# A two-layer attention and GEGLU kernel: memory denominators folded into the numerators' products, a reordered head, zeroing on GpSimd, four-bank exponentials, and a new order

## The chip, the cores and the metric

The kernel runs on one core of a Trainium2 chip. The time is device microseconds of one execution of the whole program; three runs of the kernel before gave 535.21, 535.64 and 536.88 us, a median of 535.64. One more execution was profiled. Where the text speaks of an engine, PE is TensorE (matmuls), PEld its weight loads, DVE is VectorE, ACT is ScalarE, POOL is GpSimd, and SP is the engine that issues most DMAs.

## The reference, cut to what matters

Two layers, each an attention with a compressive memory and then a gated FFN, over 2048 rows of width 512, in bfloat16.

```python
def attention(x):                       # H = 32 heads of Dh = 16, four segments of L = 512 rows
    for s in range(4):                  # one after the other: the memory is carried on
        logits = qs @ ks.T * scale + causal_mask
        a_dot = softmax(logits) @ vs
        pq = phi(qs)                    # phi(t) = t + 1 if t > 0 else exp(t)
        num = pq @ M                    # M: Dh x Dh for each head
        den = pq @ z + 1e-06            # z: Dh for each head
        o = g * (num / den) + (1 - g) * a_dot
        pk = phi(ks)
        M = M + pk.T @ vs
        z = z + pk.sum(rows)
    return concat(o) @ wo

def ffn(x):
    return gelu(x @ w_gate) * (x @ w_up) @ w_down      # inner width 1792

x = x + attention(layernorm(x))
x = x + ffn(layernorm(x))
x = x + attention(layernorm(x))
x = x + ffn(layernorm(x))
```

## The kernel before

All weights and x stay in SBUF. The work is cut into eight stages k = 0 to 7: layer one's four segments of 512 rows, then layer two's. In each stage stand the projections q, k, v (`qk`, `v`), 36 rounds of scores with their exponentials and the products of the probabilities with v (`score_round`, `flush_item`), the memory (`mem_items`, and `upd_item` which adds this segment to it), the output projection `wo`, and the FFN's `gate`, `up` and `down` products.

The heads have 16 channels, so a block of 128 channels holds eight heads. The program uses TensorE in three arrangements: `whole` (one 128x128 product), `rows` (four products side by side, one for each 32 channels: the scores) and `columns` (four products of 32 output rows each: the probabilities with v, and any dense product that happens to be issued beside them). `product` chooses `whole` or `columns` for a dense product by what stands ahead of it. A dense product is one step of 512 columns (or four steps side by side that together take the time of one).

**What sets the order.** The kernel has no hand-written sequence. The function `order` is a planner that runs while the program is built: it keeps a clock for each engine, a list of items that are ready (`Item`, each with a due time, its matmuls and what follows them), and emits the instructions in the order in which its clocks would run them. The table `POLICY`, with `STAGES` that change it in windows of 20 us of the planner's time, gives the due times, the slack of each kind of post-processing, and which engine may take a job that two or three can do. So each engine has a fixed program afterwards, and waits for others by semaphores. Where no item is ready and rounds of scores are still to come, the planner emits a small product of the tile `warm` (128 columns) as a filler.

**PSUM** is one tile `ps` of eight banks of 512 float32. An item takes one bank (`Psum`), a pair of score rounds takes two pairs of neighbouring banks, and `exp` in `score` reads one pair in one ACT instruction of 1024 elements (line 1864 of the profile). `pick` chooses a bank, `banks` holds when each comes free.

**The memory before.** After the update of stage k the tile `mblk` (four blocks of 128x128, with M on the block diagonal, made by one DVE product with the 0/1 tile `bd`, line 1286) and the tile `zcols` (four blocks of 128x8, one column for each head, line 1292) are built. In stage k + 1, `den` runs 16 products of 8 columns each into one bank (`den_mm`), DVE adds 1e-06 and multiplies by the gate (line 1195) and takes the reciprocal of 128 values (line 1200) into `rdm`; then four items `num`, one for each block of 128 channels, run four products of 128 columns each into a bank, and DVE multiplies each by `rdm` into `am` (line 1226). `am` is transposed by a DMA into `amT`, and added to the attention's output at line 1417. This happens in the six stages that have a memory.

**Other places that the change touches.** In the head, one matmul of a single row broadcasts `beta` to all partitions, between the first products of k and q. `kx` holds k with one half of its channels zeroed; its zero part is set by two DVE memsets of 1024 words (lines 707 and 709), `masked_copies` fills the rest. `vaug` is v with one more column for each head, for the softmax's sum; its column is written once by DVE (line 698). The norm's transposed rows `xnT` come from a DMA transpose or from TensorE (`turn_item`, four products with the tile `ident` and one PSUM eviction), as `turn_pe` and `turn_last` say. The last `down` item of each stage of layer two is split in two halves of 256 columns, each with its own addition to x (line 1463) and its own DMA to the output.

Of the kernel before, what the change touches and what calls it, by code (L numbers as in the profile page):

```python
# [10 lines left out]
ACT = mybir.ActivationFunctionType  # L11
ALU = mybir.AluOpType
# [20 lines left out]
SCALE = DH ** -0.5  # L33
EPS_LN = 1e-5
# [31 lines left out]
def table(halved):  # L66
# [17 lines left out]
    if halved:  # L84
# [31 lines left out]
    rs_pool=32.757, f_urge=-233.244, quick=2, paired=8, turn_pe=1, turn_last=0, w_at=29.345, w_gap=2.17,  # L116
    wd_at=78.552, wd_gap=2.776, flush_wait=-13.887, piece_slack=40.254, kb_slack=24.368, mem_slack=-20.134,
    margin=0.5, qk_due=0.962, e_q=49.408, e_k=2.993, exp_slack=-6.401, e_slack=131.01, phi_slack=22.785,
    gelu_slack=-0.789, act_evict=1.671, first_evict=0.248, gate_step=93.832, up_due=-100.529, up_step=84.355,
    down_due=-29.196, down_step=-47.297, upd_due=91.807, kb_act=82.777, vz_slack=55.93, x_dve=2.467, v0_due=-11.641,  # L120
    x1_at=-87.497, x2_at=16.051, x3_at=24.107, x3_load=-378.834, direct=2, gelu_tiles=0, look=3, lag=0.852,
    wv_at=-320.502, xn_pool=19.822, kb_pool=121.576, cut_pool=154.009, at_pool=-238.466, pe_turns=0, gate_due=4.191,
    shun=8.799, col_gap=0.807, hold=5, early=104.615, starve=0.16, near=114.234, cap=13, soon=28.208, columns=0,
    kd_slack=-5.85, zero_slack=-1.031, hold1=-49.923, hold2=2.205, hold3=11.541, hold_step=-162.485, hold_v=23.995,
    park=3)

STAGES = [
    (1, 2, dict(
        rs_pool=0.722, quick=9, kb_slack=2.193, mem_slack=-24.231, e_q=-2.643, gelu_slack=-0.49, gate_step=79.021,
        up_due=-101.483, up_step=41.973, down_step=-58.4, upd_due=91.729, vz_slack=33.291, direct=8, gelu_tiles=2,  # L130
        lag=0.412, at_pool=-237.424, early=83.209, starve=60.426, soon=7.146, park=4)),
    (2, 3, dict(
        rs_pool=2.667, quick=6, turn_pe=0, kb_slack=55.298, mem_slack=-32.756, e_q=-2.851, gelu_slack=-0.49,
        gate_step=78.038, up_due=-98.977, up_step=25.491, down_step=-53.827, upd_due=91.729, vz_slack=14.093,
        x_dve=7.459, direct=6, gelu_tiles=2, look=2.764, lag=0.475, xn_pool=30.206, cut_pool=102.189,
        at_pool=-237.424, gate_due=8.415, starve=1.292, soon=7.146, park=5)),
    (3, 4, dict(
        rs_pool=4.794, turn_pe=12, kb_slack=51.509, mem_slack=58.674, e_q=50.036, e_k=1.445, gelu_slack=1.935,
        gate_step=78.038, up_due=-96.513, up_step=85.14, down_step=-56.495, vz_slack=40.138, x_dve=6.187, direct=6,
        look=2.618, xn_pool=30.206, cut_pool=118.125, at_pool=-208.534, gate_due=14.291, shun=21.0, early=101.394,  # L140
        starve=0.321, soon=7.146, park=2)),
    (4, 5, dict(
        rs_pool=-2.341, quick=0, turn_pe=12, kb_slack=85.554, mem_slack=58.674, qk_due=1.009, e_q=50.137, e_k=1.464,
        gelu_slack=0.429, gate_step=79.294, up_due=-96.513, up_step=84.505, down_step=-72.139, vz_slack=51.333,
        x_dve=6.187, direct=3, gelu_tiles=2, xn_pool=20.238, cut_pool=148.746, at_pool=-208.534, gate_due=8.415,
        shun=21.0, early=101.394, starve=0.453, soon=7.146, park=2)),
    (5, 6, dict(
        rs_pool=36.794, quick=0, turn_pe=12, kb_slack=66.017, mem_slack=58.674, qk_due=1.009, e_q=55.15, e_k=2.984,
        gelu_slack=-0.805, gate_step=79.294, up_due=-96.513, down_step=-70.89, vz_slack=18.865, x_dve=7.455,
        gelu_tiles=2, look=2.835, lag=0.71, xn_pool=20.238, cut_pool=148.746, at_pool=-208.534, gate_due=0.276,  # L150
        shun=21.488, soon=7.146)),
    (6, 7, dict(
        rs_pool=11.417, f_urge=-261.392, quick=0, paired=11, turn_pe=0, flush_wait=0.581, piece_slack=36.524,
        kb_slack=76.591, mem_slack=-10.427, qk_due=-0.609, e_q=97.288, e_k=-5.757, exp_slack=-18.942, e_slack=69.536,
        phi_slack=30.587, gelu_slack=0.965, act_evict=1.166, gate_step=33.55, up_due=-80.509, down_due=-55.61,
        down_step=-81.567, upd_due=143.06, kb_act=60.08, vz_slack=4.039, x_dve=18.331, direct=0, gelu_tiles=2,
        look=2.622, lag=0.754, xn_pool=-3.088, kb_pool=116.679, cut_pool=153.155, at_pool=-189.709, gate_due=0.226,
        shun=85.539, hold=8, early=169.131, starve=0.31, near=101.522, cap=11, soon=0.694, kd_slack=37.99, park=6)),
    (7, 8, dict(
        rs_pool=-52.581, f_urge=-61.761, quick=3, paired=0, turn_pe=13, flush_wait=-3.039, piece_slack=92.516,  # L160
        kb_slack=220.906, mem_slack=57.517, qk_due=-30.647, e_q=-54.782, e_k=89.983, exp_slack=-17.861,
# [411 lines left out]
def order(pol, nc, cst, seg, wrk, psp, A_x, A_wq, A_wk, A_wv, A_wo, A_beta, B_x, B_w_gate, B_w_up, B_w_down, out):  # L573
# [185 lines left out]
    class Psum:  # L759
# [6 lines left out]
        def read(self, t):  # L766
            banks[self.bank] = t + 0.05
# [1239 lines left out]
```

## Time and profile before

| | |
|---|---|
| median of three runs | 535.64 us |
| span of the profiled execution, first to last instruction | 533.3 us |
| PE busy | 524.7 us, 98% |
| DVE busy | 434.6 us, 81% |
| ACT busy | 445.8 us, 84% |
| POOL busy | 252.5 us, 47% |
| DMA queue q1 | 28.20 MB, 25.8% of 16 engines' span |

The median of the runs lies 2.4 us over the profiled span. A matmul's busy time in the trace lasts from its start to its modelled end, and the next one starts long before that: a product of 512 columns is busy for 380 ns, while the starts of two that follow each other are 0.215 us apart. So PE's busy share says only that it seldom stood still; what a piece of PE's work costs is read from the starts in the timeline, as the time from a group's first start to the next group's. "issue" behind an idle time means that nothing that the profile shows was waited for.

### The profile page before, as it was taken

The page shows a single profiled execution, that of the slowest core. Times are in us where ns is not written, and L with a number is a line of the kernel's source. Part 1 is how long each engine was busy: PE and PEld are TensorE (multiplying, and loading weights), DVE is VectorE, ACT ScalarE, POOL GpSimd, SP SyncE. Part 2 cuts the span into 40 slices and gives each one's busy share as a digit, 9 for nine tenths or more (in the row PEclk, how much of TensorE's full clock was granted, in tenths as well). Part 3 has the DMA queues.
Part 4 walks back from the last instruction along what each step waited for, and adds up shares of the span by engine and source line. Part 5 has one row for each costly group of instructions (what it writes and reads, how often), then busy time and mean ns, then how long its engine had stood idle before and what let it go on. Part 6 is the DMA issues. An engine that isn't in the chain of part 4 may idle for free.

```text
span 533.3 us, 24180 instructions
## 1 busy us (share of the span) xinstructions
PE 524.7 (98%) x10697; PEld 275.7 (52%) x10697; DVE 434.6 (81%) x836; ACT 445.8 (84%) x598; POOL 252.5 (47%) x320
## 2 busy tenths in 40 slices
PE   9999989999999999999999999999999999999997
PEld 4454455444545455555564454555555456555544
DVE  7899997999997999889987788888976997586342
ACT  6999989888999989899898899799979988952320
POOL 2987472548541966428773366391632254400000
PEclk9999999999999999999999999999999999999999
DMA  8367750333330232101221122410250132102101
GB/s 271 76 120 148 190 158 4 69 39 77 42 69 16 53 56 38 32 12 25 53 41 31 25 32 27 60 33 2 53 102 3 33 51 53 23 2 48 37 2 41
DMA packets 76762, 29.99 MB, mean 56 GB/s; under 512 B 61042, under 2 KB 76658, under 8 KB 76658
## 3 DMA queue, kind: packets, MB, share of 16 engines
q1 hardware_dynamic: 76368, 28.20, 25.8%
q8 instruction: 83, 1.36, 1.0%
q10 hardware_dynamic: 290, 0.26, 0.1%
q14 instruction: 21, 0.17, 0.1%
HBM read 9.70 MB, written 2.10 MB: 22 GB/s over the span
## 4 chain that ended last, share of the span: by engine, by line
PE 75%; DVE 5%; ACT 3%; POOL 1%; issue 1%; DMA 1%; ACTq 0%
PE ps L541 75%; ACT pt L1864 1%; DVE xn L920 1%; DVE st L856 1%; ACT gel_sb L1616 1%; POOL kx L726 1%; DVE x_sb L1463 1%; ACT gel_sb L1519 1%; POOL e L1170 1%; DMA xnT<-xn 1%; ACT gel_sb L779 0%; DVE ab L1407 0%; DVE byq L1391 0%; DVE aT L1414 0%; DVE x_sb L869 0%
## 5 line engine op out<-in xcount | busy, mean ns | idle before, releaser
L1864 ACT ACTIVATE pt<-ps 128x1024 bf16<-128x1024 f32 x288 | 279.0, 1036 | 27.5 <-PE ps L541 18.6
L1813 POOL TENSOR_SCALAR_AFFINE_SELECT pt<-pt 128x256 bf16<-128x256 bf16 (+1 forms) x192 | 112.4, 598 | 176.4 <-ACT pt L1864 173.9
L541 PE MATMUL ps<-xnT,wg_sb 128*32 128x512 bf16 (+3 forms) x1367 | 107.7, 362 | 0.2 <-DMA xnT<-xn 0.2
L541 PE MATMUL ps<-wd_sb,gel_sb 128*32 128x512 bf16 (+2 forms) x1431 | 106.1, 354 | 0.0
L541 PE MATMUL ps<-xnT,wu_sb 128*32 128x512 bf16 (+1 forms) x1252 | 103.5, 379 | 0.2 <-ACT gel_sb L1519 0.2
L1557 DVE TENSOR_TENSOR gel_sb<-gel_sb,ps 128x512 bf16<-128x512 bf16 x112 | 75.2, 684 | 30.2 <-PE ps L541 27.9
L541 PEld LDWEIGHTS <-gel_sb 128*32 128x32 bf16 (+1 forms) x1623 | 53.0, 97 | 41.4 <-issue 2.2
L541 PEld LDWEIGHTS <-wu_sb 128*32 128x32 bf16 (+1 forms) x1252 | 45.6, 97 | 45.4 <-issue 2.1
L541 PEld LDWEIGHTS <-wg_sb 128*32 128x32 bf16 (+1 forms) x1367 | 47.4, 97 | 38.7 <-issue 1.4
L1391 DVE STREAM_TRANSPOSE byq<-ps 128x512 f32<-128x512 f32 x64 | 45.3, 709 | 24.0 <-PE ps L541 23.3
L1170 POOL TENSOR_SCALAR e<-e 128x512 bf16<-128x512 bf16 x32 | 49.5, 1550 | 7.0 <-ACT e L1147 6.4
L1463 DVE TENSOR_TENSOR x_sb<-x_sb,ps 128x512 bf16<-128x512 bf16 (+1 forms) x54 | 34.1, 636 | 17.9 <-PE ps L541 17.8
L1818 POOL TENSOR_SCALAR_AFFINE_SELECT pt<-pt 64x1024 bf16<-64x1024 bf16 x32 | 38.5, 1203 | 20.7 <-ACT pt L1864 17.4
L541 PE MATMUL ps<-xnT,wk_sb 128*32 128x512 bf16 (+2 forms) x330 | 34.8, 377 | 0.7 <-ACT pt L1864 0.7
L541 PE MATMUL ps<-pt,vaug 128*32 128x256 bf16 (+2 forms) x1344 | 35.1, 239 | 0.1
L541 PE MATMUL ps<-xnT,wq_sb 128*32 128x512 bf16 (+2 forms) x339 | 34.0, 377 | 0.0
L1616 ACT ACTIVATE gel_sb<-gel_sb 128x1024 bf16<-128x1024 bf16 (+4 forms) x31 | 33.3, 1157 | 0.0
L541 PE MATMUL ps<-wv_sb,xnT 128*32 128x512 bf16 (+1 forms) x227 | 32.4, 380 | 0.8 <-DVE x_sb L1463 0.4
L541 PE MATMUL ps<-q,kx 32*128 32x64 bf16 (+2 forms) x1120 | 31.6, 217 | 0.6 <-ACT pt L1864 0.3
L541 PEld LDWEIGHTS <-vaug 128*32 128x32 bf16 x1344 | 27.1, 97 | 9.2 <-issue 1.6
L856 DVE BATCH_NORM_STATS2 st<-x_sb 128x6 f32<-128x512 bf16 x46 | 31.3, 680 | 0.4
L541 PEld LDWEIGHTS <-kx 32*128 32x128 bf16 x1120 | 17.0, 92 | 28.2 <-issue 27.4
(127 smaller groups left out, 708.7 us busy)
## 6 DMA issues: line engine op xcount, KB each, us to landing
vz<-vaug SPq DMA_DIRECT2D x14, 136.0 KB, 2.9
wg_sb<-in_B_w_gate_dram SPq DMA_DIRECT2D x8, 224.0 KB, 2.9
wu_sb<-in_B_w_up_dram SPq DMA_DIRECT2D x8, 224.0 KB, 3.9
wd_sb<-in_B_w_down_dram SPq DMA_DIRECT2D x7, 256.0 KB, 5.9
x_sb<-in_A_x_dram SPq DMA_DIRECT2D x3, 512.0 KB, 6.7
out_dram<-x_sb SPq DMA_DIRECT2D x12, 128.0 KB, 1.9
xnT<-xn SPq DMA_TRANSPOSE x56, 2.6
kx<-kf SPq DMA_DIRECT2D x12, 64.0 KB, 3.2
```

The source lines that it names most:

```text
L541: self.nc.tensor.matmul(*args, **kw)
L726: return lambda: eng.tensor_scalar(out=kx[:, :, C * which:C * which + n], in0=kf[:, :, 0:n], scalar1=masks[:, which:which + 1], scalar2=No ...
L856: nc.vector.bn_stats(out=self.st6[:, 0, :], in_=x_sb[:, self.tt0 + j, :])
L920: eng.tensor_scalar(out=xn[:], in0=x_sb[:, self.tt0 + j, :], scalar1=self.mv[:, j, 1:2] if self.wide else self.mv[:, j, 0:1], scalar2=self ...
L1170: lambda eng: eng.tensor_scalar(out=e[0][:], in0=e[0][:], scalar1=1.0, scalar2=None, op0=ALU.min), summed)
L1391: nc.vector.transpose(out=(self.byq[:, pars[0], :, :].rearrange("p a c -> p (a c)") if h is None else self.byq[:].rearrange("p u a c -> p ...
L1463: ck.dve.post(ck.made(), slack, (0.15 + 0.00104 * (c1 - c0), lambda: nc.vector.tensor_tensor(out=xt, in0=xt, in1=ps()[:, 0:c1 - c0], op=AL ...
L1557: ck.dve.post(ck.made(), NORMAL, (0.683, lambda: nc.vector.tensor_tensor(out=g, in0=g, in1=ps()[:], op=ALU.mult), lambda t: (ps.read(t), e ...
L1616: return (0.205 + 0.427 * (f1 - f0), lambda: nc.scalar.activation(out=g, in_=g, func=ACT.Gelu_apprx_tanh), lambda t: self.gelu_done(t, f0, ...
L1813: nc.gpsimd.affine_select(out=view, in_=view, pattern=[[0, 4], [0, n], [1, C]], compare_op=ALU.is_ge, fill=0.0, base=C, channel_multiplier=-1)
L1818: nc.gpsimd.affine_select(out=view, in_=view, pattern=[[0, 4 * TPS], [1, C]], compare_op=ALU.is_ge, fill=0.0, base=0, channel_multiplier=-1)
L1864: nc.scalar.activation(out=pt_all[:, s0:s0 + 2, 2 * p:2 * p + 2, :].rearrange("p r h c -> p h r c"), in_=ps_all[:, pair[0]:pair[1] + 1, :] ...
```

## The change

Denominators: the tiles `mblk` and `zcols` become one tile `mz` of four blocks of 128x136, in which each head has its 16 columns of M and one column of z. The 16 products `den_mm` are gone. The numerators' products are 136 columns wide and give the sums too. Since three blocks of 136 fit into a bank, and four don't, the four items `num` become three, of which two hold six products and one four; each takes a pair of neighbouring banks (`Pair`, `wide`). DVE then adds 1e-06 and multiplies by the gate for each item (one instruction, or two), takes a reciprocal of 48 or 32 values, and multiplies (one instruction, or two). `mz` is filled by four DVE instructions instead of one.

```diff
-                    product(ps()[:, j * P:(j + 1) * P], self.phiq[:, b, j * P:(j + 1) * P], mem_state[k - 1][0][:, b, :])
+            parts = [((0, 0, None), (1, 4, 0)), ((2, 0, None), (1, 4, 1)), ((3, 0, None),)]
+                ps = Pair()
+                    product(ps()[:, i, MZ * u:MZ * u + MZ], self.phiq[:, b, j * P:(j + 1) * P], mem_state[k - 1][0][:, b, :])
...
+                    steps = [(0.175, den(whole, 0, 2, 0, 4), None)]
+                    if half:
+                        steps.append((0.157, den(1, 2, 3, 4, 6), None))
+                    steps.append((0.454 if half else 0.354, inverse, None))
+                    if half:
+                        steps.append((0.42, scale(1, 2, 3, 4, 6, 2 * n, 2 * n + 2), None))
+                    steps.append((0.69, scale(whole, 0, 2, 0, 4, 0, TPS), told))
```

Head, zeroing and columns: `beta_row` has 128 rows, all zero but the first, and its product runs with the full tile `warm` behind the first product of q; the zero part of `kx` is set by GpSimd at the start; GpSimd may take the columns of `vaug` too.

```diff
-    beta_row = cst.tile([1, H], BF16, name="beta_row")
+    beta_row = cst.tile([P, H], BF16, name="beta_row")
+    nc.gpsimd.memset(beta_row[:], 0.0)
...
+    for kx in kxs:
+        nc.gpsimd.memset(kx.bitcast(mybir.dt.uint32)[:, :, :, C // 2:3 * C // 2], 0)
...
     a0.first_k(ps1, 0, half)
-    te.matmul(beta_ps, lhsT=warm[0:1, :], rhs=beta_row[:], start=True, stop=True)
     a0.first_q(ps2, 0, half)
+    te.matmul(beta_ps, lhsT=warm[:], rhs=beta_row[:], start=True, stop=True)
```

Four-bank exponentials: where four neighbouring banks are free, and at least `join` more, both pairs of a score round are read by one ACT instruction of 2048 elements. In the program made, this happens four times; 280 exponentials of two banks are left of 288.

```diff
+        joined = bool(runs) and len(got) - 4 >= pol.join
...
+                nc.scalar.activation(
+                    out=pt_all[:, s0:s0 + 2, :, :].rearrange("p r h c -> p h r c"),
+                    in_=ps_all[:, b0:b0 + 4, :].rearrange("p h (r c) -> p h r c", r=2), func=ACT.Exp, scale=SCALE)
```

The last `down` item of a stage of layer two is split into 384 and 128 columns, and `POLICY` and `STAGES` hold new numbers throughout, so the order on every engine is another.

```diff
-                downs[-1:] = [down(TPS - 1, 0, D // 2), down(TPS - 1, D // 2, D)]
+                downs[-1:] = [down(TPS - 1, 0, D - P), down(TPS - 1, D - P, D)]
...
-    rs_pool=32.757, f_urge=-233.244, quick=2, paired=8, turn_pe=1, turn_last=0, w_at=29.345, w_gap=2.17,
+    rs_pool=-104.717, f_urge=-62.078, quick=7, paired=14, turn_pe=0, turn_last=0, w_at=29.345, w_gap=1.105,
```

Counted over the whole programs:

| | before | changed |
|---|---|---|
| products of 8 columns for the denominators (whole, and groups of four in columns) | 64 + 32 | 0 |
| products for the numerators (whole, and groups of four) | 67 + 29, 128 columns | 28 + 68, 136 columns |
| TensorE transposes of xn (`ident`) | 32 | 48 |
| DMA transposes of xn | 56 | 52 |
| filler products of 128 columns (whole, and groups of four) | 11 + 2 | 0 + 3 |
| changes between the three arrangements | 292 | 301 |
| all dense products of q, k, v, wo, gate, up, down | the same | the same |
| ACT gelu instructions over kept tiles | 31 | 17 |
| DVE instructions | 798 | 858 |

Three places show how the instructions moved. The first is DVE at the memory of stage 1, before: `rdm` are the denominators, `am` the scaled numerators, `ab`, `aT` and `byq` belong to the attention of the stage before, `gel_sb` lines to the FFN.

```order
L1407 TENSOR_TENSOR ab<-byq,r 128x2x16x16
L1195 SCALAR_TENSOR_TENSOR rdm<-ps,tmp_e_135 128x128
L1200 RECIPROCAL rdm<-rdm 128x128
L1557 TENSOR_TENSOR gel_sb<-gel_sb,ps 128x512 x3
L1226 TENSOR_TENSOR am<-ps,rdm 128x512 x2
L1557 TENSOR_TENSOR gel_sb<-gel_sb,ps 128x512 x3
```

The same place on DVE in the changed program (line numbers are its own):

```order
L742 CAST gel_sb<-ps 128x512
L1186 SCALAR_TENSOR_TENSOR rdm<-ps,tmp_e_138 128x32
L1186 SCALAR_TENSOR_TENSOR rdm<-ps,tmp_e_138 128x16
L1194 RECIPROCAL rdm<-rdm 128x48
L1201 TENSOR_TENSOR am<-ps,rdm 128x256
L1201 TENSOR_TENSOR am<-ps,rdm 128x512
```

One denominator pass for the stage, followed by four multiplications spread between other work, has become three runs of sums, reciprocal and multiplications, and all of a run stands between the matmuls that fill a pair of banks and the moment that the pair comes free.

The second place is PE at the end of stage 0, where the rows of the first FFN's norm are turned on TensorE (`ident`), before: `wv_sb` is a projection of v, `warm` a filler, `kx` a round of scores.

```order
L541 MATMUL ps<-wv_sb,xnT 128x512
L541 LDWEIGHTS warm
L541 MATMUL ps<-warm 128x128
...
L545 LDWEIGHTS xn
L545 MATMUL ps<-ident,xn 128x128
...
L541 LDWEIGHTS kx_123
L541 MATMUL ps<-q,kx_123 128x64
```

And in the changed program:

```order
L498 LDWEIGHTS xnT
L498 MATMUL ps<-wv_sb,xnT 128x512
...
L502 LDWEIGHTS xn
L502 MATMUL ps<-ident,xn 128x128
...
L498 LDWEIGHTS wg_sb
L498 MATMUL ps<-xnT,wg_sb 128x512
```

Before, eleven fillers stand around the last transposes, and the gate's first products come after a round of scores and the memory's update; now the last eight transposes follow a projection of v and the gate's first products follow them, with no filler.

The third place is the end of the program, on DVE, before (`x_sb` lines add a `down` product to x):

```order
L1557 TENSOR_TENSOR gel_sb<-gel_sb,ps 128x512 x14
L1463 TENSOR_TENSOR x_sb<-x_sb,ps 128x512 x3
L1463 TENSOR_TENSOR x_sb<-x_sb,ps 128x256 x2
```

And in the changed program:

```order
L1559 TENSOR_TENSOR gel_sb<-gel_sb,ps 128x512 x14
L1465 TENSOR_TENSOR x_sb<-x_sb,ps 128x512 x2
L1465 TENSOR_TENSOR x_sb<-x_sb,ps 128x384
L1465 TENSOR_TENSOR x_sb<-x_sb,ps 128x128
L1465 TENSOR_TENSOR x_sb<-x_sb,ps 128x512
```

The split item is no longer the last one: behind its 128 columns comes a whole item of 512.

More of the change, by code (lines that the diff above doesn't have):

```diff
@@ L531, in __init__ @@
         self.posted, self.chain = 0.0, False
[L532 removed]
+        self.early, self.rest, self.stop, self.wide = None, None, 0, False
 class Products:
@@ L1806, in open_item @@
         items.remove(it)
+        if it.wide:
+            bank = min(free_pairs(), key=lambda p: max(banks[p[0]], banks[p[1]]))[0]
+            banks[bank + 1] = 1e9
         it.ps.bank = bank
@@ L1921, in order @@
             for ck.back in (pol.lag, 0.0):
-                got = [it for it in items if it.after in ev and it.ready() and (
+                got = [it for it in items if it.after in ev and (not it.wide or free_pairs()) and it.ready() and (
                     it.kind != "flush" or it.chain or not streams or tight() or it.posted < late or ck.mode == "columns")]
```

521 lines of the change are left out of this document (261 added, 260 removed).

## The prediction

> **What bounds the kernel now.** First the page: which engine is busy, and what the chain that ended last is made of.
>
> ```profile
> span 533.3 us, 24180 instructions
> PE 524.7 (98%) x10697; PEld 275.7 (52%) x10697; DVE 434.6 (81%) x836; ACT 445.8 (84%) x598; POOL 252.5 (47%) x320
> PE 75%; DVE 5%; ACT 3%; POOL 1%; issue 1%; DMA 1%; ACTq 0%
> ```
>
> PE is the engine that sets the end. The other engines are four fifths busy, near enough to matter where they are late, but a microsecond more on DVE or ACT costs nothing by itself. Next the busy time by stretches, to see where PE stood still and at what clock.
>
> ```profile
> core 0: us, PE busy (x) PEld busy (x) DVE busy (x) ACT busy (x) POOL busy (x), PEclk, DMA share, GB/s
> 0.00:20.00 20.00, 18.77 (x134) 8.88 (x135) 15.91 (x49) 15.59 (x32) 10.17 (x23) 1.00 0.71 204
> 20.00:40.00 20.00, 19.68 (x386) 10.09 (x388) 17.66 (x38) 19.89 (x31) 17.34 (x23) 1.00 0.54 107
> 40.00:60.00 20.00, 19.28 (x486) 10.26 (x475) 17.84 (x34) 19.92 (x25) 13.39 (x19) 1.00 0.75 165
> 60.00:80.00 20.00, 18.28 (x361) 9.70 (x359) 18.56 (x39) 17.42 (x30) 12.04 (x13) 1.00 0.59 165
> 80.00:100.00 20.00, 19.78 (x364) 10.04 (x366) 15.37 (x27) 19.50 (x24) 3.84 (x7) 1.00 0.12 29
> 100.00:140.00 40.00, 39.30 (x858) 19.55 (x851) 37.91 (x78) 34.27 (x48) 27.29 (x32) 1.00 0.35 56
> 140.00:200.00 60.00, 59.47 (x1189) 30.96 (x1188) 54.72 (x108) 57.02 (x77) 32.25 (x39) 1.00 0.25 48
> 200.00:300.00 100.00, 99.85 (x1984) 53.56 (x1983) 86.82 (x157) 90.37 (x111) 54.52 (x66) 1.00 0.16 31
> 300.00:400.00 100.00, 99.90 (x2194) 52.71 (x2193) 84.11 (x160) 90.49 (x124) 52.86 (x64) 1.00 0.27 44
> 400.00:480.00 80.00, 80.00 (x1736) 42.27 (x1738) 63.56 (x111) 69.09 (x82) 28.84 (x40) 1.00 0.15 28
> 480.00:533.00 53.00, 50.36 (x1044) 27.71 (x1036) 22.13 (x42) 12.27 (x23) 0.00 (x0) 1.00 0.13 32
> ```
>
> The granted clock is 1.00 throughout, so no term below has a clock in it. PE's idle time outside the first and last rows is 0.32 + 0.72 + 1.72 + 0.22 + 0.70 + 0.53 + 0.15 + 0.10 = 4.5 us; the largest piece, 1.72 us, lies between 60 and 80 us. These are the visible gaps; a gap that is shorter than a matmul's pipelined rest is hidden in the busy time. So there are two ways to make this kernel faster: less work on PE, worth its time directly, and fewer gaps, worth 4.5 us and a little more. The largest gap's stretch, in PE's timeline:
>
> ```profile
> 66.24 0.40 PE L541 MATMUL ps<-q,kx 32*128 32x64 bf16 x20
> 66.57 0.82 PE L541 MATMUL ps<-wv_sb,xnT 128*128 128x512 bf16 x3
> 67.23 0.61 PE L545 MATMUL ps<-ident,xn 128*128 128x128 bf16 x8
> 67.68 1.03 PE L541 MATMUL ps<-wv_sb,xnT 128*128 128x512 bf16 x4
> 68.54 0.33 PE L541 MATMUL ps<-warm 128*128 128x128 bf16 x3
> 71.58 0.29 PE L541 MATMUL ps<-q,kx 32*128 32x64 bf16 x7 [0.26 <-ACT pt L1864]
> 74.56 0.29 PE L541 MATMUL ps<-q,kf 16*128 16x64 bf16 x7
> 76.09 0.36 PE L541 MATMUL ps<-q,kf 16*128 16x192 bf16 x5 [1.24 <-issue]
> ```
>
> Fillers run at 68.54; at 71.58 PE waits for an exponential, and before 76.09 it stands for 1.24 us for nothing that the profile shows. The same rows give prices, from start to start. Four products of 512 columns take 68.54 - 67.68 = 0.86 us, 0.215 each. A transpose takes (67.68 - 67.23) / 8 = 0.056. The twenty score products from 66.24 are five groups of four side by side, four of 64 columns and one of 256, together the columns of one 512 product; they last 0.33 us, so the change of arrangement behind them is worth about 0.33 - 0.215 = 0.11 us.
>
> **The change, part by part.** *Denominators on PE.* Two of the six blocks, one in columns and one whole:
>
> ```profile
> 89.76 0.68 PE L541 MATMUL ps<-zcols,phiq 128*32 128x8 bf16 x64
> 90.28 0.84 PE L541 MATMUL ps<-xnT,wu_sb 128*32 128x512 bf16 x12
> 145.06 0.55 PE L541 MATMUL ps<-zcols,phiq 128*128 128x8 bf16 x16
> 145.47 1.67 PE L541 MATMUL ps<-xnT,wg_sb 128*128 128x512 bf16 x7
> ```
>
> A block takes 0.52 us in columns and 0.41 whole. With 32 groups in columns (two blocks) and 64 whole products (four blocks) that is 2 x 0.52 + 4 x 0.41 = 2.7 us, all gone. The numerators' 96 steps grow by 8 columns; at 0.215 us for 512 columns that is 96 x 8 x 0.00042 = 0.3 us added. Of all terms this is the surest, because PE has no slack to hide it.
>
> *Denominators on DVE.* The rows:
>
> ```profile
> L1226 DVE TENSOR_TENSOR am<-ps,rdm 128x512 bf16<-128x512 f32 x24 | 15.9, 678 | 1.0 <-PE ps L541 1.0
> L1200 DVE RECIPROCAL rdm<-rdm 128x128 f32<-128x128 f32 x6 | 5.7, 953 | 0.2
> L1195 DVE SCALAR_TENSOR_TENSOR rdm<-ps,tmp_e 128x128 f32<-128x128 f32 x6 | 1.7, 278 | 0.0
> L1401 DVE RECIPROCAL r<-byq 128x32 f32<-128x32 f32 x32 | 11.3, 354 | 1.1
> L1463 DVE TENSOR_TENSOR x_sb<-x_sb,ps 128x256 bf16<-128x256 bf16 x8 | 3.3, 418 | 3.9 <-PE ps L541 3.9
> ```
>
> Before: 6 x (0.278 + 0.953) + 24 x 0.678 = 23.7 us. Now: 30 narrower additions of at most 0.278 (I take 0.2), 12 reciprocals of 48 values between 0.354 and 0.953 (on the line between them, 0.45), 6 of 32 at 0.354, 18 multiplications at 0.678 and 12 half ones at the 0.418 of the other 256-wide row: 6.0 + 5.4 + 2.1 + 12.2 + 5.0 = 30.7 us, 7 us more. It is hidden behind PE as long as nobody waits for it: 434.6 + 7 is still 83% of the span. If that cover is gone, the price is the wait for banks, below.
>
> *Arrangements and transposes.* The order has 301 changes of arrangement against 292: 9 x 0.11 = +1.0 us. It has 16 more TensorE transposes: 16 x 0.056 = +0.9 us. Four DMA transposes less save PE nothing.
>
> *Head.* The one-row product of beta:
>
> ```profile
> 7.68 0.60 PE L541 MATMUL ps<-xnT,wk_sb 128*128 128x256 bf16 x4
> 8.21 0.18 PE L541 MATMUL ps<-beta_row,warm 1*128 1x32 bf16 x1
> 8.33 1.05 PE L541 MATMUL ps<-xnT,wq_sb 128*128 128x256 bf16 x8
> ```
>
> From 7.68 to 8.33 are 0.65 us for 1056 columns, which at 0.00042 us are 0.44: 0.2 us go to the arrangement of one row. With 128 rows they are saved: -0.2. The zeroing on POOL and the columns there take work from DVE in the first 40 us, where DVE isn't the bound; I cost them at nothing, between -0.2 and +0.2 (POOL's work from its start to 20 us is 10.17 us, so there is room).
>
> *Four-bank exponentials.* Four times one instruction of 2048 elements for two of 1024. ACT may gain or lose some tenths at each and the first pair's banks come free up to one exponential later; four of 144 rounds, nothing.
>
> *Tail.* Now the last item is a whole one:
>
> ```profile
> 527.35 0.69 DVE L1463 TENSOR_TENSOR x_sb<-x_sb,ps 128x512 bf16<-128x512 bf16 x1 [2.33 <-PE ps L541]
> 530.41 0.42 DVE L1463 TENSOR_TENSOR x_sb<-x_sb,ps 128x256 bf16<-128x256 bf16 x1 [1.11 <-PE ps L541]
> out_dram<-x_sb SPq DMA_DIRECT2D x12, 128.0 KB, 1.9
> out_dram<-x_sb SPq DMA_DIRECT2D x8, 64.0 KB, 1.9
> ```
>
> The addition behind the last matmul takes 0.69 instead of 0.42 us, and the last DMA 1.9 either way: +0.3.
>
> *Sum of what can be counted:* -2.7 + 0.3 + 1.0 + 0.9 - 0.2 + 0.3 = -0.4 us. The folding, worth 2.4 us alone, is nearly spent on arrangements and transposes.
>
> *Gaps.* The new order decides the rest. Its only sign outside the clock is the fillers, which stand where nothing was ready: 11 + 2 before, 3 now, and none where the first FFN begins. I take the gain as this place alone: the 1.72 us of idle between 60 and 80 us and eleven fillers at 0.056, together -2.3 us, and leave the other gaps as they are. The bounds are all 4.5 us of gaps and the fillers, -5.1, and on the other side the waits for banks, +4.9.
>
> So the span goes from 533.3 to 533.3 - 0.4 - 2.3 = 530.6 us; the runs' median lies 2.4 us over the profiled span, which gives **532.9 us**, 0.5% less.
>
> The 1.24 us gap has a rival reading. In this row the DMA queue of the instructions fetches 16 KB blocks, one each 533 / 83 = 6.4 us:
>
> ```profile
> q8 instruction: 83, 1.36, 1.0%
> ```
>
> If the gap is a block that came late beside the weight loads (165 GB/s in that stretch), the new order runs into the same late block and saves 1.24 us less: 532.9 + 1.2 = 534.1. The Trainium skill (Runtime: NRT & Kernel Launch, section Instruction fetch mechanics) says that fetching is hidden, since instructions are dispatched more slowly than blocks are filled; by that rule the gap is something else in this order, and the 532.9 holds. No row here shows what PE waited for.
>
> **The rivals.** *Only the count shows (no gap is won).* The new order moves the gaps instead of closing them: 535.6 - 0.4 = 535.2 us. For it: the other engines are as busy as before, ACT at 19.9 of 20 us until 60 us, and the same exponentials must be done. Against: no fillers are left there.
>
> *Banks (slower).* A numerator item now holds two neighbouring banks until DVE has done a whole run: two additions, a reciprocal and two multiplications, 0.4 + 0.45 + 0.418 + 0.678 = 2.0 us for twelve of them, 0.2 + 0.354 + 0.678 = 1.2 us for six; before, one bank was held for 0.678. The additional hold is 12 x 1.3 + 6 x 0.5 = 19 us on a pair, plus what queues ahead on DVE. Behind a bank wait are dense products and, through the pairs, score rounds, and ACT with them. If a quarter of it shows as waiting PE, that is +4.9 us, and with the count and no gap won 535.6 - 0.4 + 4.9 = 540.1. It decides from 2.0 us on, 0.11 us for each of the 18 items, if no gap is won. The Trainium skill (TensorEngine Tiling (Array Packing), section Gotcha 1: PSUM Pressure) warns that row tiling raises the pressure on PSUM because its tiles write to different banks; that is why four banks go with each score round here. Against this rival: six banks are left beside a pair, and PE waits for ACT's or DVE's banks only for tenths in the rows above.
>
> *All gaps close:* 535.6 - 0.4 - 5.1 = 530.1 us. Against: some of these gaps are chains through norm and transposes that no order removes.
>
> **How the numbers follow.** Chances: the forecast with its neighbourhood, 531.0 to 534.0, 0.50; all gaps close, 0.12; only the count, with the late block's 534.1, 0.20; banks or a new wait like them, 0.18. A measurement of this kernel can't tell less than 0.3%, 1.6 us, from no change: faster means below 534.0, slower above 537.2. So faster is 0.50 + 0.12 = 0.62, the same 0.20, slower 0.18. The range is 529.5, just under all gaps closed, to 538.0, which takes in a mild form of the bank wait; beyond it I leave about 0.1 above and less below. The forecast's own range is 531.0 to 534.0.
>
> **What would show it.** The denominators' 8-column products are gone and the products of `mz` start about 0.058 us apart in both arrangements, which confirms the first term; if they start further apart, it is wrong. Between 60 and 80 us PE's idle should fall from 1.72 to under 0.5 us; if it doesn't, the gap term is wrong and the time is 535. The sum of idle over 20 to 480 us should be about 2.7; if it is over 6, with waits of PE for `am` or for the exponentials behind the pairs of banks, the bank rival has it. The last addition takes 0.69 us. DVE should be busy for 435 to 447 us.

## The result, and the profile after

The changed kernel is slower: 554.70 us, the median of four runs (553.64 to 556.98), against 536.05 for the kernel before on the same chip. The ratio is 1.036 with an interval of 1.032 to 1.040. The forecast was 532.9, with a range up to 538.0. The profiled execution took 554.22 us, with a span of 552.5. Its page, first lines and the chain that ended last, by engine:

```profile
span 552.5 us, 24098 instructions
...
PE 526.9 (95%) x10652; PEld 271.2 (49%) x10652; DVE 433.7 (78%) x899; ACT 442.3 (80%) x590; POOL 244.4 (44%) x316
...
PE 67%; ACT 15%; DVE 8%; issue 4%; DMA 4%; POOL 1%; SPq 0%; ACTq 0%; DVEq 0%; POOLq 0%
```

PE's busy time hardly moved (524.7 before, 526.9 now). The 19.2 us that the span grew by are nearly all idle PE: 552.5 - 526.9 = 25.6 us against 8.6. The other engines did the same work and were idle longer too, so none of them became the bound; in the chain PE's share fell from 75% to 67%, and what took its place are ACT, DVE and DMAs that PE waited for. By stretches, with the columns of the prediction's view (span of the stretch, busy us of PE, PEld, DVE, ACT and POOL, clock, DMA):

```profile
40.00:60.00 20.00, 18.15 (x341) 8.69 (x343) 16.15 (x30) 18.25 (x25) 10.72 (x14) 1.00 0.76 174
60.00:80.00 20.00, 17.00 (x390) 8.79 (x386) 17.31 (x32) 18.03 (x23) 13.00 (x18) 1.00 0.43 127
...
140.00:200.00 60.00, 56.69 (x1072) 28.44 (x1070) 47.20 (x103) 47.08 (x62) 27.52 (x30) 1.00 0.21 34
200.00:300.00 100.00, 96.38 (x1958) 49.48 (x1958) 81.94 (x169) 87.32 (x119) 44.62 (x55) 1.00 0.20 37
300.00:400.00 100.00, 94.83 (x2063) 48.06 (x2065) 81.68 (x179) 83.57 (x110) 50.89 (x63) 0.98 0.20 37
```

The loss isn't at one place. From 200 to 400 us, where PE had stood still for 0.25 us in the kernel before, it now stands for 3.62 + 5.17 = 8.8 us. What it waited for, over the whole execution (us in total, times, longest), is the next view:

```profile
PE ps L498 <- DMA xnT<-xn: 9.7, 7, 2.6
PE ps L498 <- issue: 2.3, 1, 2.3
PE ps L498 <- ACT pt L1876: 2.1, 4, 1.1
PE ps L498 <- POOL pt L1824: 1.5, 1, 1.5
...
PE ps L498 <- ACT gel_sb L743: 1.0, 1, 1.0
PE ps L498 <- DMA phik<-e: 0.7, 1, 0.7
...
PE ps L502 <- DVE am L1201: 0.6, 1, 0.6
```

Before, the line for the DMAs that write `xnT` was this one:

```profile
PE ps L541 <- DMA xnT<-xn: 0.2, 1, 0.2
```

So 9.5 of the 17.0 us of new idle time, over half, are PE waiting for the transposed rows of a norm. The longest of these waits, in PE's timeline, and under it the DMAs on SP's queue in the same stretch:

```profile
336.08 0.70 PE L498 MATMUL ps<-vaug,phik 128*32 128x32 bf16 x64
336.60 0.25 PE L498 MATMUL ps<-warm 128*32 128x128 bf16 x4
339.47 1.05 PE L498 MATMUL ps<-wv_sb,xnT 128*32 128x512 bf16 x16 [2.62 <-DMA xnT<-xn]
```

```profile
335.23 6.19 SPq L711 DMA_TRANSPOSE xnT<-xn  x4
```

SP began to issue the four transposes of this norm at 335.23 and was through with the last at 341.4. PE had come to the values' product of the first block of these rows at 336.85 and stood 2.62 us until that block had landed. In these traces PE's products run in the order of the program, so all that was placed behind it stood too. The wait was made by the order: the product was put there too early.

**The numbers in the new table that do this.** The table's full text holds two numbers that the shortened diff above doesn't show. `margin` is added to the time at which the planner takes a DMA transpose as landed; it was 0.5 us everywhere. `lag` is taken off PE's time when the planner asks whether an input is there; it lay between 0.0 and 1.4.

```diff
-    margin=0.5, ...                                  (whole table; lag from 0.004 to 1.414)
+    margin=-4.735, ...                               (base)
+    margin 0.5, 0.5, 1.409, 0.297                    (planner's 0 to 80 us)
+    margin=-5.965 ... -2.498 ... -56.548 ... -4.811  (stretches behind it)
+    lag=-32.215, -31.838, -46.448                    (planner's 40 to 100 us; 0.85 to 37.9 elsewhere)
```

With a margin of -4.7 a transpose counts as landed as soon as SP has issued it. In the stretch above the first block landed 4.2 us after its issue had begun, and 2.62 us of that show as PE's wait.

**How far the chip falls behind the plan.** The planner has a clock of its own, by which it places every instruction; it is code of the kernel and no measurement. Set against the trace, matmul by matmul in program order, it shows where the chip loses time that the planner did not count on; the time that the planner itself leaves empty ("holes") is in both and drops out. In us, chip minus plan, the median of the matmuls around each time of the trace, and at the end the span minus the planner's last time:

```
at us of the trace     40    80   120   160   200   250   300   350   400   450   500    end
kernel before         0.3   1.1   1.4   2.5   2.9   2.9   2.9   2.7   2.9   2.7   2.7    4.9   (plan 528.4)
the change           -0.1   4.2   4.2   9.6   9.4  10.7  13.8  18.9  20.0  20.4  21.4   25.1   (plan 527.4)
```

By the planner's clock the change gains 1.0 us. On the chip it falls back by 20.2 us more than the kernel before, in steps at the waits listed above.

### The profile page after: what moved, and what is told of

Read it like the earlier page. It is cut to its first block, busy times and chain, and to the rows that moved or that the text cites. A ratio compares the mean times of both kernels' runs of the same rounds, so it can differ in the third digit from the quotient of the medians.

```text
span 552.5 us, 24098 instructions
## 1 busy us (share of the span) xinstructions
PE 526.9 (95%) x10652; PEld 271.2 (49%) x10652; DVE 433.7 (78%) x899; ACT 442.3 (80%) x590; POOL 244.4 (44%) x316
## 4 chain that ended last, share of the span: by engine, by line
PE 67%; ACT 15%; DVE 8%; issue 4%; DMA 4%; POOL 1%; SPq 0%; ACTq 0%; DVEq 0%; POOLq 0%
PE ps L498 66%; ACT pt L1876 7%; DMA xnT<-xn 4%; ACT gel_sb L1618 3%; ACT gel_sb L1521 2%; DVE x_sb L1465 1%; ACT L540 1%; ACT e L1111 1%; DVE byq L1393 1%; DVE xn L884 1%; POOL xn L884 1%; DVE x_sb L833 0%; DVE st L820 0%; DVE gel_sb L1559 0%; DVE phiq L1115 0%
## 5 line engine op out<-in xcount | busy, mean ns | idle before, releaser
L1876 ACT ACTIVATE pt<-ps 128x1024 bf16<-128x1024 f32 x280 | 267.5, 1043 | 31.8 <-PE ps L498 28.1
L1819 POOL TENSOR_SCALAR_AFFINE_SELECT pt<-pt 128x256 bf16<-128x256 bf16 (+1 forms) x192 | 114.5, 610 | 206.5 <-ACT pt L1876 181.1
L498 PE MATMUL ps<-xnT,wg_sb 128*32 128x512 bf16 (+2 forms) x1451 | 107.4, 378 | 6.8 <-issue 2.3
L498 PE MATMUL ps<-xnT,wu_sb 128*32 128x512 bf16 (+1 forms) x1210 | 105.0, 380 | 0.6 <-DVE gel_sb L1559 0.4
L498 PE MATMUL ps<-wd_sb,gel_sb 128*32 128x512 bf16 (+4 forms) x1497 | 103.1, 357 | 0.0
L1465 DVE TENSOR_TENSOR x_sb<-x_sb,ps 128x512 bf16<-128x512 bf16 (+2 forms) x51 | 32.4, 636 | 22.0 <-PE ps L498 21.8
L1824 POOL TENSOR_SCALAR_AFFINE_SELECT pt<-pt 64x1024 bf16<-64x1024 bf16 x24 | 28.5, 1188 | 12.3 <-ACT pt L1876 10.6
L498 PE MATMUL ps<-wo_sb,aT 128*32 128x512 bf16 (+1 forms) x311 | 31.3, 380 | 0.0
L820 DVE BATCH_NORM_STATS2 st<-x_sb 128x6 f32<-128x512 bf16 x43 | 29.2, 678 | 0.3
```

The costliest lines, as they stand in the source:

```text
L498: self.nc.tensor.matmul(*args, **kw)
L820: nc.vector.bn_stats(out=self.st6[:, 0, :], in_=x_sb[:, self.tt0 + j, :])
L1465: ck.dve.post(ck.made(), slack, (0.15 + 0.00104 * (c1 - c0), lambda: nc.vector.tensor_tensor(out=xt, in0=xt, in1=ps()[:, 0:c1 - c0], op=AL ...
L1819: nc.gpsimd.affine_select(out=view, in_=view, pattern=[[0, 4], [0, n], [1, C]], compare_op=ALU.is_ge, fill=0.0, base=C, channel_multiplier=-1)
L1824: nc.gpsimd.affine_select(out=view, in_=view, pattern=[[0, 4 * TPS], [1, C]], compare_op=ALU.is_ge, fill=0.0, base=0, channel_multiplier=-1)
L1876: nc.scalar.activation(out=pt_all[:, s0:s0 + 2, 2 * p:2 * p + 2, :].rearrange("p r h c -> p h r c"), in_=ps_all[:, pair[0]:pair[1] + 1, :] ...
```

## The experiments

**Theory M**: `margin` is the cause; the planner places products ahead of rows that have not landed. **L**: `lag` is. **B**: the code is (the pairs of banks, the new products, the zeroing on POOL). **D**: any table but the old one falls behind like this.

*1. margin put back in the changed table, e1_after_margin.*

```diff
-    margin=-4.735, ... margin=-5.965, ... margin=-4.811 (13 places)
+    margin=0.5 (all)
```

> The changed kernel with one number of its table put back: margin, which is added to the time at which the planner takes a DMA transpose as landed, is 0.5 everywhere as in the kernel before (the changed table has -4.735, -4.811, -5.965, -56.548 and others). Theory M (the planner is told that transposed rows land some 5 us early, and puts TensorE's products ahead of them): TensorE's wait on the DMAs that write xnT falls from 9.7 us to under 2 us and no dip of the granted clock is left. The order that results has more holes, filled with transposes of ident (about 180 such rows against 3), so the sum of streaming and changes of arrangement rises by about 13 us, and the time is 542 to 552 us. Theory L (lag, the other number that moves a product against its input, is the cause) and theory B (banks held in pairs): the wait on the DMAs stays at 7 us or more, and the time is 560 us or more, since the holes come on top.

Measured: 591.38 us, ratio 1.103 [1.099, 1.107]. That is far above the 542 to 552 us of theory M, and the wait on `xnT` fell to 7.4 us in two pieces, not to under 2. By the letter this is what was forecast for theories L and B: a wait of 7 us or more, and over 560 us.

```profile
PE ps L498 <- ACT pt L1876: 10.3, 17, 4.5
PE ps L498 <- DMA xnT<-xn: 7.4, 2, 5.7
```

But the planner's clock now ends at 580.7, 53 us later, where 13 had been expected: the table's other numbers were chosen with the false margin, and without it the planner itself finds holes. Against its plan the chip behaves as theory M says: it is 4.9 us behind at 120 us and 5.5 at 500, where the change went from 4.2 to 21.4. The 5.7 us wait stands in the plan as well (at 540 us the chip is 5.7 us behind). The waits alone don't tell planned holes from surprises; the distance to the plan does, and the next runs are read by it.

*2. The false margin in the kernel before, e2_before_margin.* Code and all other numbers unchanged.

```diff
-    margin=0.5, qk_due=0.962, ...
+    margin=-4.8, qk_due=0.962, ...
```

> The kernel before, code and table, with margin -4.8 in place of 0.5. Theory M: TensorE's wait on the DMAs that write xnT rises from 0.2 us to 6 to 12 us, in gaps of 0.5 to 3 us in front of products that read xnT, and the time from 536 us to 543 to 552 us (order alone: 12 more changes of arrangement and 4 more fillers, about 1.5 us). Theories L, B and D (the new code, or other numbers of the table): the wait stays under 2 us and the time is 536 to 539 us.

Measured: 552.82 us, 1.032 [1.028, 1.036], 0.8 us above the range given; this is as slow as the change, with nothing of its code. The plan ends at 533.4, 5.0 us later than unaltered, and the chip is 17.4 us behind it, 12.5 us more. The wait is in the expected range:

```profile
PE ps L541 <- DMA xnT<-xn: 7.8, 9, 2.1
```

So one number is enough to make such a loss, and the new code isn't needed for it.

*3. The new code with the old table, e3_code_alone.* `join` and `col_pool`, which the old table lacks, are set so that no four-bank exponential is formed and the columns stay on DVE; `margin` is 0.6.

> The changed kernel's code with the table of the kernel before (margin 0.6). Theory B (the paired banks, the new products or the masked k on GpSimd stall TensorE): waits for pt and am of 5 us or more in all, and 550 us or more. Theory M: TensorE waits on xnT's DMAs under 1.5 us, on the evictions of the pairs under 3 us; the old numbers suit the new code badly and leave holes (about 134 fillers against 13, some 6 us), so 540 to 545 us, well under the 554 us of the change.

Measured: 566.35 us, 1.056 [1.053, 1.060]. By the letter this is theory B's result: over 550 us, and the waits for `pt` are 7.8 us.

```profile
PE ps L542 <- ACT pt L1920: 7.2, 15, 1.4
...
PE ps L542 <- DMA xnT<-xn: 1.8, 2, 1.5
```

None is for `am`, though, and the planner saw the waits coming: its clock ends at 559.4, and the chip is 5.7 us behind. My count of fillers had valued the holes of an unsuited table at 6 us; by the planner's clock they are 31. Experiment 5 decides on B.

*4. lag put back as well, e4_after_margin_lag.* As the first, and `lag` 0.852 in place of values below 0 or above 3.

> As the first of these runs, and lag also put to 0.852 where the changed table has values below 0 or above 3. Theory L: against the first run the waits for evictions and for the DMAs fall further, and the time by 5 us or more. Theory M: within 4 us of the first run, since lag matters only where margin has let the product go ahead; the order has about as many holes (203 fillers), so 543 to 554 us.

Measured: 607.13 us, 1.133 [1.128, 1.137]; the plan ends at 586.4. Both forecasts of the time are missed: it rose by 15.8 us against the first experiment. Two things can be read. At 120 us the chip is 0.1 us ahead of the plan, where it was 4.9 behind in the first experiment: the false `lag` between 40 and 100 us costs in that stretch. And near 290 us a surprise comes with both numbers put back, so honest numbers don't rule all of them out; SP's, DVE's and PE's timelines:

```profile
290.64 1.19 SPq L711 DMA_TRANSPOSE amT<-am  x1
291.94 5.15 SPq L711 DMA_TRANSPOSE phik<-e  x4
```

```profile
290.19 0.42 DVE L1419 TENSOR_TENSOR aT<-aT,amT 128x512 bf16<-128x512 bf16 x1
```

```profile
294.42 0.22 PE L498 MATMUL ps<-vaug,phik 128*32 128x32 bf16 x4 [6.95 <-DMA phik<-e]
```

The transpose into `amT` starts when DVE's last reader of that buffer has run; four transposes into `phik` stand behind it on SP, and PE stands for 6.95 us for them. That the first waited for this reader is read from the times, not tested.

*5 and 6. The new code, unaltered, with tables chosen anew under an honest margin, e5_refit and e6_refit_other.*

```diff
-    margin=-4.735 ..., lag=-46.448 ... 37.889
+    margin=0.5, lag 0.0 to 2.5, the other numbers chosen anew
```

> The changed kernel's code, unaltered, with another table: margin is 0.5 everywhere, lag lies between 0 and 2.5, and the other numbers were chosen anew until the planner's own clock (it is code of the kernel and no measurement) ended about where it ends with the changed table: 528.6 us against 527.4 for the change and 528.4 for the kernel before. Theory M (the planner is told of inputs before they are there): the chip falls behind the planner's clock by 4 to 8 us as in the kernel before (4.9) and not by 25 as in the change, so the span is 532.5 to 536.5 and the time 535 to 539 us; TensorE's wait on the DMAs that write xnT is under 2 us. Theory B (the paired banks, the new products, the masked k on GpSimd): the code is the same, so the time stays at 550 us or more. Theory D (the chip falls behind any table but the old one by about 17 to 25 us): 548 us or more.

> A second such table for the same code, reached by another path, with margin 0.5 and lag from 0 to 2.5, whose planner's clock ends at 528.8 us. Theory M: again 4 to 8 us behind the planner's clock, 535 to 539 us. Theories B and D: 548 us or more. If the two tables fall behind by amounts more than 4 us apart, the planner's clock misses something besides the landings, which the waits of the later one have to show.

Measured: 537.69 us, 1.0036 [1.0002, 1.0070], and 541.38 us, 1.0102 [1.0069, 1.0136]. The first is in theory M's range, the second 2 us above it; both are 13 us or more below the change with the same code. B and D, which gave 548 us or more, fall. Two other parts of theory M's forecast were missed: the chip was 9.3 and 11.8 us behind the plan at the end, not 4 to 8, and in experiment 5 the wait on `xnT` was 3.1 us, not under 2. In experiment 5, 4.5 of the 9.3 us had come about by 80 us and only 2.1 us came from there to 500 us. The place is above all one wait and 3.4 us of halved clock behind it (last section); its waits view, PE's timeline and SP's:

```profile
PE ps L602 <- DMA xnT<-xn: 3.1, 3, 2.0
PE ps L602 <- ACT pt L1980: 1.7, 6, 0.4
```

```profile
56.50 0.52 PE L602 MATMUL ps<-xnT,wq_sb 128*128 128x512 bf16 x1 [1.97 <-DMA xnT<-xn]
```

```profile
50.86 0.60 SPq L662 DMA_DIRECT2D wg_sb<-in_B_w_gate_dram  x1
51.50 0.59 SPq L1123 DMA_DIRECT2D kx<-kf  x1
52.20 1.24 SPq L815 DMA_TRANSPOSE xnT<-xn  x1
53.48 0.58 SPq L662 DMA_DIRECT2D wu_sb<-in_B_w_up_dram  x1
```

A transpose issued at 52.20 between loads of the weights was there for PE at 56.5, 4.3 us later; the planner, with a margin of 0.5, had it earlier. Experiment 6 has the same wait at the same place, 3.3 us long.

*7 and 8. In the table of experiment 5, one false number at a time from 160 us on.* The order up to there is the same in all three.

```diff
 (e7)  margin=-4.8 from 160 us of the planner's clock
 (e8)  lag=-32.0   from 160 us of the planner's clock
```

> The table of the first new one (run e5_refit), with margin -4.8 in place of 0.5 from 160 us of the planner's clock on; code, other numbers and the whole order up to 160 us are the same. The planner's clock ends at 533.9 us, so the new order by itself is worth 5.3 us more than e5's 528.6. Theory M: behind 160 us the chip falls back by another 7 to 12 us, as it did in the change (from 9.5 us at 160 us to 22) and in e2; the span is 533.9 + 9.3 (what e5 fell back in all) + 7 to 12 = 550 to 555 us, the time 551 to 557 us, and TensorE waits for the DMAs that write xnT, phik or amT for 4 us or more behind 160 us. Theory D (any order but a fitted one falls back): about the same as the next run.

> As the run before, but with lag -32 from 160 us on (the planner takes whatever is under way as done) and margin left at 0.5. The planner's clock ends at 534.9 us. Theory M: lag lets a product go ahead of the end of an eviction or of an exponential, and of a landing only within the last 0.2 us, so the chip falls back by less than with margin: 0 to 5 us behind 160 us, with waits for ACT and DVE of some tenths each; time 545 to 550 us. Theory L: 7 us or more, 553 us or above, and more than in the run before.

Measured: 551.31 us, 1.028 [1.023, 1.033], and 559.26 us, 1.042 [1.037, 1.048]. The distance to the plan, with experiment 5 beside them:

```
at us of the trace       40    80   120   160   200   250   300   350   400   450   500    end
e5_refit                0.2   4.5   4.5   5.1   5.1   5.8   5.7   6.0   5.9   6.0   6.6    9.3   (plan 528.6)
e7_refit_margin        -0.1   3.7   3.8   6.1   6.6   9.1  10.1  10.3  13.7  14.3  13.8   16.1   (plan 533.9)
e8_refit_lag            0.0   1.8   2.0   2.4   4.1   6.0   8.1   8.9  11.2  15.1  16.6   22.6   (plan 534.9)
e9_refit_head           0.1   0.1   0.4   3.1   3.4   3.6   4.6   5.2   5.2   6.0   6.1    8.5   (plan 530.9)
```

From 160 to 500 us the honest table loses 1.5 us to its plan, the false margin 7.7, the false lag 14.2; another 5.3 and 6.3 us of the longer times are in the plans. The margin did what theory M said. On lag theory M was wrong, with 0 to 5 us, and L was right that it does more harm than the margin. The waits of e7, then of e8:

```profile
PE ps L608 <- DMA xnT<-xn: 7.1, 6, 1.8
...
PE ps L608 <- DMA phik<-e: 1.1, 2, 0.6
```

```profile
PE ps L607 <- POOL pt L1933: 8.9, 8, 1.7
...
PE ps L607 <- DMA xnT<-xn: 4.4, 3, 2.0
```

With lag at -32 a flush is placed ahead of the masks that POOL still has to write into `pt`, and waits for POOL up to 1.7 us, eight times. I had thought of evictions alone, which end within tenths. Both numbers do the same thing: they tell the planner that an input is there before it is.

*9. An honest table with more room beside the weight loads, e9_refit_head.*

> A third new table for the same code: margin 3.0 from 40 to 60 us of the planner's clock, 1.5 in the 20 us on either side and 0.5 elsewhere, other numbers chosen anew; the planner's clock ends at 530.9 us. In e5 the chip fell back by 4.5 us between 40 and 80 us, at one wait of 2.0 us on the DMA that writes xnT (issued between loads of the weights) and at the halved clock behind it. If a landing that is late beside the weight loads is the cause, this wait is under 0.7 us now, no halved clock is left there, the chip is less than 2.5 us behind the planner at 80 us and 4 to 6.5 us behind it at the end: span 535 to 537.5, time 536.5 to 540 us. If the fall-back there has another cause, it stays at 4 us or more and the time is 541 us or more.

Measured: 541.21 us, 1.0097 [1.0075, 1.0120], 1.2 us above the range, and the chip is 8.5 us behind the plan at the end, not 4 to 6.5. The time alone would fit the other forecast, 541 us or more; the distance at 80 us does not. The mechanism was right where it was meant to act: no wait for `xnT` is left in the view of waits, and the chip is 0.1 us behind at 80 us against 4.5. The largest new loss, 2.7 us against the plan, lies between 120 and 160 us:

```profile
132.69 0.28 PE L575 MATMUL ps<-q,kx 32*128 32x64 bf16 x14
134.47 0.20 PE L575 MATMUL ps<-q,kx 32*128 32x64 bf16 x2 [1.51 <-issue]
...
136.70 0.61 PE L575 MATMUL ps<-q,kx 32*128 32x256 bf16 x11 [0.94 <-ACT pt L1971]
```

PE stops for 1.51 us in the middle of a group of score products, which wait for nothing that the view names. Then it waits 0.94 us for one of the four-bank exponentials (line 1971), and the clock is half from 136.16 to 139.57.

The kernel before has such a stop of 1.24 us, which the prediction quoted, and experiment 4 has one of 1.17 us before 127.36. One account fits all three. PE's instructions come by DMA in the blocks of 16 KB that the prediction shows, 83 in the kernel before, and by the slope in these traces a block holds 255 to 256 of them. A block lands in each of these stops, at 74.77, 133.03 and 125.95 us. By then PE had run 442, 444 and 442 matmuls and weight loads more than 256 for each block before it, the most in each trace; at no other landing in the eleven traces is the count over 428. PE goes on 1.3 to 1.5 us behind the landing. So PE seems to have run out of loaded instructions. This is read from counts; no run tested it.

## Why the prediction was wrong

*The counted terms were right.* The products of `mz` were expected 0.058 us apart. In PE's timeline of the change, six of them and what follows:

```profile
88.89 0.52 PE L498 MATMUL ps<-mz,phiq 128*128 128x136 bf16 x6
89.25 1.89 PE L498 MATMUL ps<-xnT,wg_sb 128*128 128x512 bf16 x8
```

That is (89.25 - 88.89) / 6 = 0.060, with no 8-column products left. In columns, four groups take from 310.84 to 311.08, 0.060 each as well. The beta product in PE's timeline:

```profile
8.21 0.60 PE L498 MATMUL ps<-xnT,wq_sb 128*128 128x256 bf16 x4
8.64 0.18 PE L498 MATMUL ps<-beta_row,warm 128*128 128x32 bf16 x1
8.67 0.60 PE L498 MATMUL ps<-xnT,wq_sb 128*128 128x256 bf16 x4
```

and DVE's last row:

```profile
549.00 0.69 DVE L1465 TENSOR_TENSOR x_sb<-x_sb,ps 128x512 bf16<-128x512 bf16 x1 [2.73 <-PE ps L498]
```

Four products and the beta row now take 8.67 - 8.21 = 0.46 us, 0.2 less than the 0.65 before, as the sum had it; the addition takes the 0.69 that was forecast. Adding up PE's columns and changes of arrangement over the whole order at the prices of the prediction (0.215 us for 512 columns, 0.11 for a change, 0.41 and 0.52 for the blocks of 8-column products) gives about 1.2 us less than before: the sum's terms on PE, -0.7, and 0.5 for the ten fillers fewer. A four-bank exponential takes 1.88 us, two of two banks 2 x 1.04: a fifth of a microsecond gained at each. Only DVE's total was off: 433.7 us, just under the 435 to 447 expected. The denominators' rows on it did grow as the sum had it, from 23.3 to 30.1 us (forecast 30.7), but other rows shrank, such as `xn` from 25.4 to 21.3 us. Little hung on that: PE waits for DVE for under 3 us in all outside the start.

*The bank rival was not what happened.* PE waits 0.6 us for `am` and 2.1 for exponentials. The forecast's test for this rival asked for over 6 us of idle with such waits; the idle came (19.5 us from 20 to 480 us) with 2.7 us of them, and experiment 5 has the same pairs at 537.69 us. The chance of 0.18 also covered "a new wait like them". New waits did come, but for transposed rows, by another mechanism than that rival's, and with 17 us of idle in place of its 4.9.

*The step that failed is the gap term.* It said that "the new order decides the rest" and that "its only sign outside the clock is the fillers", took eleven fillers and the gap of 60 to 80 us as gained, and left "the other gaps as they are". There were other signs: `margin` and `lag` in the table that makes the order. Few fillers meant only that the planner believed something was ready. Between 60 and 80 us PE's idle rose from 1.72 to 3.00 us, where under 0.5 was forecast. The term was -2.3 us; in its place the chip lost 20.2 us to the plan. Of the 1.72 us taken as gained there, 1.24 were the stop that the prediction could not name. The counts under experiment 9 fit its other reading, the late instruction block, so that by them fetching is not hidden at that place. The changed kernel has no such stop; that piece was gained, and more was lost beside it.

Of these 20.2 us, read from the waits and the distance to the plan:

- Behind 80 us, PE stood 1.10 + 0.40 + 1.43 + 1.30 + 2.62 + 0.99 us for `xnT` and 0.7 for `phik`, 8.5 us in all, and a halved clock behind the longest wait cost 1.7 us (below). In all these places the table's margin was false; experiments 2 and 7 show that such a margin is enough for a loss of this kind, and experiment 1 that without it the distance stops growing. That each single wait comes from it is argued, not tested.
- Up to 80 us the chip fell back 3.1 us more than before. 1.85 us are a late landing near 48 us, in a stretch where the margin was honest; experiments 5 and 6 have this too, and 9 removes it. 1.5 us are a wait for POOL's mask in the stretch with the false lag, the kind that experiment 8 shows.
- At 141.56 us PE stood 2.34 us, put down to "issue". The product there reads all four transposed blocks. The last of them was issued at 138.89 and landed 4.9 us later, at 143.8; the product started at 143.91. By these times the stop is one more wait for `xnT`.
- The remainder, 20.2 - 8.5 - 1.7 - 3.1 - 2.3 = 4.6 us, are waits for ACT and DVE of 0.3 to 1.1 us each (1.05 for `pt` at 317 us, 1.0 for `gel_sb`, 0.6 each for `x_sb` and `am`) and pieces too short to name. They weren't taken apart.

*What stays open.* The changed program has 1.2 us less for PE to do by the count, but no table tried here shows a gain: the best is level with the kernel before within 0.7%. Whether another one would isn't settled.

## What to carry to other kernels

Where a planner sets the order, read first the numbers that say when an input counts as there; an optimistic one makes the plan look full and turns into waits at the head of an in-order queue. Set the plan's clock beside the trace, in program order: the places where the distance grows are the surprises, and the waits that lie in the plan drop out. A count of fillers or of instructions says nothing about such waits, so a term that rests on the order alone deserves a range as wide as the landings it relies on.

## What the hardware showed that was not expected

**Stalls well under 3.4 us can halve PE's clock.** In the change, three stretches around the longest wait; the clock is the third column from the end:

```profile
334.00:337.30 3.30, 2.85 (x141) 1.89 (x140) 2.95 (x9) 3.14 (x8) 2.92 (x3) 1.00 0.23 47
337.30:340.70 3.40, 1.23 (x32) 0.68 (x36) 2.40 (x6) 1.15 (x3) 1.08 (x2) 1.00 0.45 75
340.70:344.10 3.40, 3.40 (x44) 1.07 (x40) 0.74 (x2) 2.39 (x6) 0.00 (x0) 0.51 0.40 80
```

Behind the stretch in which PE was busy for 1.23 of 3.40 us, the clock is half for the next 3.4 us; half of that, an estimate of 1.7 us, is lost. It is not the length of the wait that decides. Experiments 5 and 8 run the same order up to 160 us and have the same wait, 1.97 and 2.02 us; the first falls to half clock and the second doesn't:

```profile
53.20:56.60 3.40, 1.13 (x30) 0.61 (x23) 3.21 (x5) 3.40 (x5) 2.19 (x2) 1.00 1.11 138
56.60:60.00 3.40, 3.18 (x8) 1.18 (x8) 1.29 (x2) 0.16 (x1) 0.88 (x2) 0.50 0.81 184
```

```profile
53.60:57.00 3.40, 1.33 (x7) 0.60 (x7) 2.27 (x4) 2.29 (x3) 2.59 (x4) 1.00 0.69 140
57.00:60.40 3.40, 3.40 (x90) 1.76 (x88) 2.14 (x4) 2.35 (x3) 0.00 (x0) 1.00 0.88 245
```

PE was busy for 1.13 us of its stretch in the one, 1.33 in the other. This share doesn't decide either. In experiment 7 a stretch with 2.35 us of work, in which no single stop is over 0.65 us, is followed by half clock:

```profile
135.16:138.58 3.42, 2.35 (x50) 1.22 (x42) 3.02 (x6) 3.24 (x5) 3.29 (x3) 1.00 0.45 76
138.58:141.99 3.41, 3.27 (x60) 1.86 (x60) 0.18 (x1) 1.63 (x3) 3.24 (x6) 0.50 0.02 5
```

What decides stays open. The stretches themselves lie on a fixed grid: in experiments 6 and 7 the two halved ones start 81.92 us apart (58.53 and 140.45 in experiment 6), 24 times 3.413. So the same stall can fall differently on them. The Trainium skill (TensorE: Matmul & The Clock Gate, section What's actually happening) says that the activity is judged over free-running windows of 3413 ns, and the lengths here agree. Its section HAM oscillation — how this bites in real kernels gives as the rule that idle gaps of over about 3.4 us are to be avoided; here 2.0 and 2.62 us were enough, and the measurement decides.
